# Down products of expert units 1 to 14, group 0: from four block products of 512 columns to seven products of sums of 256

## The chip, the cores and the metric

The kernel runs on one core of one Trainium2 chip. The metric is device microseconds (us) of one execution. TensorE (PE; PEld is its weight load) does the matrix products, VectorE (DVE), ScalarE (ACT) and GpSimd (POOL) work on rows of 128 partitions, and SyncE (SP) issues the transfers. PSUM is the memory that TensorE writes, in banks of 512 float32 columns.

## The reference, cut to what matters

A retention layer comes first, then a gated layer with 1536 hidden columns, then four experts with 1024 hidden columns each, all of whose outputs are summed with the weights `p`. The change is in the second product of the experts.

```python
def _moe2_ref(x, domain_probs, w1, w2):          # x: 1536 x 512, from the gated layer
    p = domain_probs / (domain_probs.sum(-1, keepdims=True) + 1e-09)
    out = np.zeros((N, D), dtype=np.float32)
    for e in range(E):                           # E = 4, F = 1024 hidden columns
        h = np.maximum(x @ w1[e], 0.0)
        out += p[:, e:e + 1] * (h @ w2[e])
    return out.astype(np.float32)
```

## The kernel before

The 1536 tokens are two groups `g` of 768, and a group is two blocks of 384 (three tiles of 128 tokens each). The 4 x 1024 hidden columns are 16 units `u` of 256, two parts `f` of 128. Every float32 operand is split into a high part `hi` (fp32r, rounded by a copy on ScalarE) and a low part `lo` (the rest, a subtraction on VectorE or GpSimd), and a product is three matmuls: hi x hi, hi x lo, lo x hi.

The expert stage walks through the steps (u, g). A step has two halves:

- `hidden_products` runs `winograd`: the hidden block of 256 columns x 768 tokens comes from seven products of sums in place of eight block products. Each is six matmuls of 384 columns (L463). They come in the order 1, 2, 5, 6, 3, 7, 4, and here they are p1, p2, p5, p6, p3, p7, p4. Products 1, 5 and 6 are copied out of PSUM (`kept`, L472, ScalarE), and the others are added to such a copy (L1036, VectorE). `expert_use` then makes the four operands `hs` by relu (L1039, L1027) with their low parts (L1043, L1029).
- `expert_out` makes the down product: six outputs of 128 tokens x 512 columns, each from two parts f by three matmuls of 512 columns (L1071 to L1073): 36 matmuls. VectorE adds each, times `p`, onto `oacc` (L1079).

A generator for the down product of a step (`before` in the last loop) is run between the products of the next step: p1, p2, three outputs, p5, p6, p3, p7, three outputs, p4. Thus TensorE's order is written out by hand. What the other engines do, and in which order, is set while the program is written by `Pace`: it holds assumed costs of each engine, and `fill` hands waiting tasks (level 0 first) to the engine that would be free; a task for `"PV"` may go to GpSimd or VectorE, and GpSimd is asked first. Each engine then executes its list strictly in order.

Weights: `piece_tasks` loads a piece into one of `STAGED` = 2 staging buffers, casts the high part (L380), and subtracts the low part (L385); for the up weights ("1", u) it also makes four sums (L352). Up weights take turns in three big places (`BIG`), the down weights ("2", u) have two small ones.

Of the kernel before, what the change touches and what calls it, by code (L numbers as in the profile page):

```python
# [15 lines left out]
P = 128  # L16
# [146 lines left out]
def tile_retention_gated_experts(  # L163
# [46 lines left out]
    N1 = DFF // FU  # L210
    UPE = F // FU
    N2 = E * UPE
    STAGED = 2
    BIG = 3
    SMALL = 2
    BANKS = 6
    WARM = 8

# [26 lines left out]


    pieces = []
    n_big = n_small = 0

    def wide(key, w, c0):  # L250
        nonlocal n_big
        rows = w.rearrange("(h j p) f -> j p h f", p=P, j=KH)
        for j in range(KH):
            pieces.append((key, j, rows[j, :, :, c0:c0 + FU], n_big))
        n_big += 1

    def plain(key, w, r0):
        nonlocal n_small
        for j in range(NF):
            pieces.append((key, j, w[r0 + j * P:r0 + (j + 1) * P, :].rearrange("p (h f) -> p h f", h=2), n_small))  # L260
            n_small += 1
# [14 lines left out]
    used = {"big": set(), "small": set()}  # L276
    pools = {}

    def is_wide(key):
        return key[0] in "gv1"  # L280

    def has_slot(n):
        key, j, _, slot = pieces[n]
        kind, size = ("big", BIG) if is_wide(key) else ("small", SMALL)
        pool = ("big", slot % BIG) if is_wide(key) else "small"
        return pool in pools and (slot < size or slot - size in used[kind])

    def w_used(key):
        kind = "big" if is_wide(key) else "small"
        used[kind].update(x[3] for x in pieces if x[0] == key)  # L290

    ready = {}
    open_weights = [False]
    stage_free, ones, tops, sums_done, highs = [], [[], []], [], [], []
    bits_pools = {0: psum_bits}

    def piece_tasks(n):

        key, j, src, slot = pieces[n]
        double = src.dtype == I64  # L300

        second = n % 2 if n >= 4 else 0
# [59 lines left out]

        def high_part(eng, half):
            if is_wide(key) and j == half == 0:
                assert has_slot(n)
                i = slot % BIG
                wt[key] = [
                    pools["big", i].tile([P, 7, KH, P], F32R, tag=f"big{part}{i}", name=f"wide{part}{i}", bufs=1)
                    for part in ("hi", "lo")
                ]  # L370
            elif not is_wide(key):
                assert has_slot(n)
                i = slot % SMALL
# [29 lines left out]
        for half in range(2 if is_wide(key) else 1):  # L403
            size = 384 if is_wide(key) and half == 0 else NC
            last = source
            if half == 1:
                for i in range(4):
                    before = sums_done[-1:] if i == 0 else []
                    last = then("PV", P, lambda eng, i=i: sums(eng, i), last, *before)
            hi = then(  # L410
                "A", size, lambda eng, half=half: high_part(eng, half), last, *highs[-1:], gate=lambda: has_slot(n)
            )
            highs.append(hi)
            lows.append(then("PV", size, lambda eng, half=half: low_part(eng, half), hi))
        if is_wide(key):
            sums_done.append(lows[-1])
        if double:
            tops[-1][0].extend(lows)
        stage_free.append(taken if double else lows)
        ready.setdefault(key, []).extend(lows)  # L420

    for n in range(len(pieces)):
        piece_tasks(n)

    def weights(key):
        pace.matmuls(0, pace.need(*ready[key]))
        return wt[key] if is_wide(key) else [wt[key + (f,)] for f in range(NF)]

    pools["big", 0] = pools["big", 1] = wring

# [493 lines left out]
    accp = ctx.enter_context(tc.tile_pool(name="accp", bufs=1))  # L924
    pools["big", 2] = inner

    turn = [0]

    def any_tile():

        n = turn[0] % 14
        turn[0] += 1
        if n < 4:
            silu_places.next()
            return tp.tile([P, TB], F32R, tag="s", name="hs", bufs=4)
        return pools["hp"].tile([P, TB], F32R, tag=("hhi", "hlo")[n % 2], name="hs")

    x2 = [None] * G
    x2_tasks = [{"X": [], "T": []} for _ in range(G)]
# [82 lines left out]

    def expert_use(hs):
        def use(f, blk, a, b):
            hi, lo = any_tile(), any_tile()
            if b is None:
                nc.scalar.activation(out=hi, in_=a, func=AF.Relu)  # L1027
                end = pace.did("A", TB)
                nc.vector.scalar_tensor_tensor(  # L1029
                    out=lo, in0=a, scalar=0.0, in1=hi.bitcast(F32), op0=ALU.max, op1=ALU.subtract  # L1030
                )
                end = pace.did("V", TB, end)
                hs[f, blk] = hi, lo, pace.done(end)
# [13 lines left out]
            readers += [high, low]  # L1047
            hs[f, blk] = hi, lo, low
            return end
        return use  # L1050

    def expert_out(u, g, hs):
        e = u // UPE
        w = weights(("2", u))
        if u == 0:
            oacc.append(accp.tile([P, 2 * CPB, DM], F32, tag=f"acc{g}", name=f"oacc{g}"))
        for n in range(2 * CPB):
# [8 lines left out]
            for half in range(halves):  # L1066
                cols = slice(half * DM // halves, (half + 1) * DM // halves)
                ps = bank()[:, cols]
                for f in range(NF):
                    (whi, wlo), (hi, lo, _) = w[f], hs[f, blk]  # L1070
# [12 lines left out]
                if u == N2 - 1:  # L1083
                    nc.sync.dma_start(out=out[tt * P:(tt + 1) * P, cols], in_=acc)
            if g == G - 1 and n == 2 * CPB - 1:
                w_used(("2", u))
            pace.fill(3 * NF * 0.216)
            yield

    first = {}  # L1090

    def hidden_products(u, g, hs):
        if u == 0:
            pace.matmuls(0, pace.need(*x2_tasks[g]["X"]))
        return winograd(weights(("1", u)), x2[g], expert_use(hs))

# [3 lines left out]
    for i, (u, g) in enumerate(steps):  # L1100
# [26 lines left out]
        if i == 5:  # L1127
            nc.vector.tensor_reduce(out=p_sum, in_=p_raw, axis=mybir.AxisListType.X, op=ALU.add)
            nc.vector.tensor_scalar(out=p_sum, in0=p_sum, scalar1=PEPS, scalar2=None, op0=ALU.add)
            nc.vector.reciprocal(out=p_sum, in_=p_sum)  # L1130
            nc.vector.tensor_tensor(out=p_sb, in0=p_raw, in1=p_sum.to_broadcast([P, NTT, E]), op=ALU.mult)
            pace.did("V", 300)
    for u in range(N2):
# [79 lines left out]
```

## Time and profile before

| | |
|---|---|
| time, median of 3 runs | 863.73 us (862.88 to 865.69) |
| profiled execution: its own time | 866.24 us |
| span of the profiled execution | 864.4 us, mean granted TensorE clock 1.000 |
| PE busy | 851.0 us (98%), 4731 matmul records |
| PEld busy | 792.9 us (92%) |
| DVE busy | 576.3 us (67%) |
| ACT busy | 379.7 us (44%) |
| POOL busy | 280.7 us (32%) |
| chain that ended last | 88% of the span on PE |

The span is first to last instruction on the core; the execution's own time is 1.8 us longer. Busy time of PE is modelled, so 98% does not say that it streams at its peak; the start times of its matmuls do say how fast they follow one another.

### The profile page before, as it was taken

The numbers are of one execution on the slowest core, as the hardware profiler recorded it, in microseconds if no ns is written. First come the engines' busy times: TensorE is split into PE (matmuls) and PEld (weight loads), VectorE is DVE, ScalarE is ACT, GpSimd is POOL, SyncE is SP. The second block draws the span as 40 slices with busy tenths as digits, with TensorE's granted clock in tenths as the row PEclk, the third lists the DMA queues.
The fourth block names the chain that finished last, engine by engine and source line by source line (L and its number), as shares of the span: only waits on it lengthen the run. The fifth ranks groups of instructions, "written<-read, shape, count | busy, mean of one in ns | idle before, by whom it ended". The sixth has DMA issues, their size and how long they took to land.

```text
span 864.4 us, 12619 instructions
## 1 busy us (share of the span) xinstructions
PE 851.0 (98%) x4731; PEld 792.9 (92%) x4731; DVE 576.3 (67%) x1054; ACT 379.7 (44%) x845; POOL 280.7 (32%) x354
## 2 busy tenths in 40 slices
PE   9989999999999999999999999999999999999998
PEld 8889999999999999889889998999899988999897
DVE  3987878979977876943665656556656556555554
ACT  3877765544344456655233233333233333333221
POOL 1366666525244458651122112012012112201000
PEclk9999999999999999999999999999999999999999
DMA  7762133221212111101011011001001101101003
GB/s 233 255 201 95 50 98 89 69 64 49 74 50 84 63 50 36 37 25 37 13 49 37 13 50 43 31 25 50 25 25 49 36 13 49 37 16 47 25 8 139
DMA packets 32749, 52.74 MB, mean 61 GB/s; under 512 B 4358, under 2 KB 13446, under 8 KB 32688
## 3 DMA queue, kind: packets, MB, share of 16 engines
q1 hardware_dynamic: 32480, 51.70, 19.1%
q8 instruction: 37, 0.61, 0.3%
q10 hardware_dynamic: 208, 0.23, 0.1%
q14 instruction: 24, 0.20, 0.1%
HBM read 48.78 MB, written 3.15 MB: 60 GB/s over the span
## 4 chain that ended last, share of the span: by engine, by line
PE 88%; DVE 5%; ACT 3%; POOL 2%; issue 2%; DVEq 0%; ACTq 0%; POOLq 0%
PE bank L463 41%; PE bank L1072 10%; PE bank L1073 10%; PE bank L1071 10%; PE bank L1004 3%; PE bank L1005 3%; PE bank L1003 3%; PE bank L676 2%; PE bank L668 1%; DVE s L556 1%; PE bank L648 1%; POOL x2Tlo L956 1%; DVE kept L553 1%; PE state L704 1%; PE bank L829 0%
## 5 line engine op out<-in xcount | busy, mean ns | idle before, releaser
L1079 DVE SCALAR_TENSOR_TENSOR oacc<-bank,p_sb,oacc 128x512 f32<-128x512 f32 (+1 forms) x181 | 135.0, 746 | 66.5 <-PE bank L1073 66.5
L1073 PE MATMUL bank<-plainhi,hs 128*128 128x512 f32 (+1 forms) x386 | 151.0, 391 | 0.0
L1072 PE MATMUL bank<-plainlo,hs 128*128 128x512 f32 (+1 forms) x386 | 151.0, 391 | 0.0
L1071 PE MATMUL bank<-plainhi,hs 128*128 128x512 f32 (+1 forms) x386 | 149.7, 388 | 0.0
L472 ACT COPY kept<-bank 128x384 f32<-128x384 f32 x168 | 80.8, 481 | 152.3 <-PE bank L463 150.4
L1036 DVE TENSOR_TENSOR kept<-bank,kept 128x384 f32<-128x384 f32 x96 | 53.5, 558 | 119.1 <-PE bank L463 94.9
L385 POOL TENSOR_TENSOR plainlo<-wst,plainhi 128x512 fp32r<-128x512 f32 x16 | 27.8, 1739 | 283.3 <-ACT plainhi L380 283.3
L463 PE MATMUL bank<-x2Thi,widehi 128*128 128x384 f32 x256 | 86.4, 338 | 0.7 <-DVE kept L1036 0.7
L463 PE MATMUL bank<-x2Thi,widelo 128*128 128x384 f32 x256 | 86.3, 337 | 0.0
L1073 PEld LDWEIGHTS bank<-plainhi,hs 128*128 128x128 f32 x386 | 72.5, 188 | 15.1
L463 PE MATMUL bank<-x2Tlo,widehi 128*128 128x384 f32 x256 | 86.0, 336 | 0.0
L1072 PEld LDWEIGHTS bank<-plainlo,hs 128*128 128x128 f32 x386 | 72.4, 187 | 14.1 <-POOL plainlo L385 0.3
L385 POOL TENSOR_TENSOR widelo<-sums,widehi 128x512 fp32r<-128x512 f32 x37 | 48.4, 1309 | 112.7 <-ACT widehi L380 112.3
L1071 PEld LDWEIGHTS bank<-plainhi,hs 128*128 128x128 f32 x386 | 72.5, 188 | 13.5
L1039 ACT ACTIVATE hs<-kept 128x384 fp32r<-128x384 f32 x96 | 50.6, 527 | 76.4 <-DVE kept L1036 76.4
L1004 PE MATMUL bank<-hlo,plainhi 128*128 128x384 f32 x192 | 64.4, 335 | 1.1 <-POOL hlo L561 1.0
L463 PE MATMUL bank<-xThi,widehi 128*128 128x384 f32 x192 | 64.6, 336 | 0.0
L463 PE MATMUL bank<-xThi,widelo 128*128 128x384 f32 x192 | 64.2, 334 | 0.0
L463 PE MATMUL bank<-xTlo,widehi 128*128 128x384 f32 x192 | 64.2, 334 | 0.0
L1005 PE MATMUL bank<-hhi,plainlo 128*128 128x384 f32 x192 | 64.2, 334 | 0.0
L1003 PE MATMUL bank<-hhi,plainhi 128*128 128x384 f32 x192 | 64.1, 334 | 0.0
L561 POOL TENSOR_TENSOR hlo<-s,hhi 128x384 fp32r<-128x384 f32 x44 | 47.0, 1071 | 33.4 <-ACT hhi L558 26.7
(155 smaller groups left out, 1925.9 us busy)
## 6 DMA issues: line engine op xcount, KB each, us to landing
wst<-in_moe_w_dram SPq DMA_DIRECT2D x64, 256.0 KB, 2.8
wst<-in_moe_w_gate_dram SPq DMA_DIRECT2D x12, 512.0 KB, 3.8
wst<-in_moe_w_val_dram SPq DMA_DIRECT2D x12, 512.0 KB, 3.7
wst<-in_moe_w_out_dram SPq DMA_DIRECT2D x12, 512.0 KB, 3.3
v<-in_vn_dram SPq DMA_DIRECT2D x12, 256.0 KB, 3.5
kn<-in_kn_dram SPq DMA_DIRECT2D x12, 256.0 KB, 3.9
q<-in_qt_dram SPq DMA_DIRECT2D x11, 256.0 KB, 4.4
k<-in_kt_dram SPq DMA_DIRECT2D x11, 256.0 KB, 3.1
```

Of the source, the lines that this page charges most:

```text
L385: eng.tensor_tensor(out=at(lo), in0=t, in1=at(hi).bitcast(F32), op=ALU.subtract)
L463: nc.tensor.matmul(out=ps, lhsT=lhs, rhs=rhs, start=(first and j == i == 0), stop=(j == KH - 1 and i == 2), skip_group_check=not first,)
L472: nc.scalar.copy(out=t, in_=ps)
L1003: nc.tensor.matmul(out=ps, lhsT=whi[:, c], rhs=hi, start=(f == 0), stop=False)
L1004: nc.tensor.matmul(out=ps, lhsT=whi[:, c], rhs=lo, start=False, stop=False)
L1005: nc.tensor.matmul(out=ps, lhsT=wlo[:, c], rhs=hi, start=False, stop=(f == NF - 1))
L1036: nc.vector.tensor_tensor(out=t, in0=a, in1=t, op=ALU.add)
L1039: 0, "A", TB, lambda eng: eng.activation(out=hi, in_=t, func=AF.Relu), [pace.done(end)]
L1071: nc.tensor.matmul(out=ps, lhsT=hi[:, c], rhs=whi[:, cols], start=(f == 0), stop=False)
L1072: nc.tensor.matmul(out=ps, lhsT=hi[:, c], rhs=wlo[:, cols], start=False, stop=False)
L1073: nc.tensor.matmul(out=ps, lhsT=lo[:, c], rhs=whi[:, cols], start=False, stop=(f == NF - 1))
L1079: nc.vector.scalar_tensor_tensor(out=acc, in0=ps, scalar=pe, in1=acc, op0=ALU.mult, op1=ALU.add)
```

## The change

The down product of group 0 is made by seven products of sums in units 1 to 14 (`MIXED`). The 256 x 512 down weights of a unit are four blocks of 128 x 256, the hidden block of 256 columns x 768 tokens four blocks of 128 x 384. Seven operands of hidden sums and seven of weights (four of them sums, `T`) are multiplied: for each product three tiles of 128 tokens, three matmuls each, of 256 columns. That is 63 matmuls of 256 columns in place of 36 of 512. The products are in the order 1, 4, 6, 5, 7, 3, 2; here they are m1, m4, m6, m5, m7, m3, m2. Group 1 and units 0 and 15 stay as they were.

Around it: `mixed_use` keeps the relu as float32 (`h`), makes four differences of such tiles, and splits seven operands in place of four. `down_sums` makes the four sums of down weights and splits them. `mixed_out` accumulates products in three banks and in two `cross` banks, which were used only for the weights' bits earlier, and adds each of the five partial results onto `oacc`, two of them in halves of 256 columns. After such a unit, TensorE takes the products of group 1's hidden block and the sums' products in turn, one of each (p1', m1, p2', m4, p5', m6, p6', m5, p3', m7, p7', m3, p4', m2; a dash marks group 1). There are three staging buffers, the third big place holds the down weights of odd units, up weights have two places, and down weights are loaded right behind the up weights of their own unit.

```diff
@@ constants and order of the loads
-    STAGED = 2
+    HD = DM // 2
+    MORE_HS = 2
+    MIXED = set(range(1, N2 - 1))
+    STAGED = 3
...
-    for u in range(N2):
-        turns += wides[2 * N1 + u + 1:2 * N1 + u + 2] + [plains[N1 + u]]
+    turns += [wides[2 * N1 + 1], plains[N1], plains[N1 + 1]]
+    for u in range(2, N2):
+        turns += [wides[2 * N1 + u], plains[N1 + u]]
...
@@ new: sums of the down weights
+        def sums(eng, i):
+            t1, t2, t3, t4 = tiles()
+            (b11, b12), (b21, b22) = of(upper), of(lower)
+            o, x, y = ((t1, b12, b11), (t2, b22, t1), (t3, b22, b12), (t4, b21, t2))[i]
+            eng.tensor_tensor(out=o, in0=x, in1=y, op=ALU.subtract)
...
@@ new: mixed_use, on group 0's hidden block
+        def operand(n, t, dep):
+            hi, lo, tags = pair()
+            high = pace.add(0, "A", TB, lambda eng: eng.copy(out=hi, in_=t), [dep])
+            low = pace.add(
+                0, "PV", TB, lambda eng: eng.tensor_tensor(out=lo, in0=t, in1=hi.bitcast(F32), op=ALU.subtract), [high]
+            )
...
+            elif at == (1, 1):
+                operand(4, t, done[at])
+                done[5] = sub(h[0, 1], h[0, 1], t, ALU.add, done[7], done[at])
+                done[6] = sub(h[0, 0], h[0, 1], h[0, 0], ALU.subtract, done[5], *read[1])
+                operand(5, h[0, 1], done[5])
+                operand(6, h[0, 0], done[6])
...
@@ new: mixed_out
+        plan = (
+            (1, plain_part(0, low_half), cross, lambda c: c != 1, (0, low_half, cross)),
+            (4, sum_part(3), left, lambda c: True, None),
+            (6, sum_part(1), cross, None, (0, high_half, cross)),
+            (5, sum_part(0), right, lambda c: False, (1, every, both)),
+            (7, sum_part(2), cross, None, (1, every, cross)),
+            (3, plain_part(1, high_half), right, None, None),
+            (2, plain_part(1, low_half), left, lambda c: True, (0, every, both)),
+        )
...
@@ the last loop
-            if not start:
+            if mixed:
+                hidden = hidden_products(u, g, hs, True)
+                for _ in range(7):
+                    next(hidden)
+                    next(before)
+            elif not start:
...
-            before = expert_out(u, g, hs)
+            mixed = is_mixed(u, g)
+            before = (mixed_out if mixed else expert_out)(u, g, hs)
```

What this does to the engines' lists is shown at three places of the steady stretch. First TensorE, between the last output of a down product and p4 of the next hidden block, before (L1071 to L1073 are an output's matmuls, L463 those of p4):

```order
L1071 MATMUL bank<-plainhi_7046,hs 128x512
L1072 MATMUL bank<-plainlo_7047,hs 128x512
L1073 MATMUL bank<-plainhi_7046,hs 128x512
L463 MATMUL bank<-x2Thi_4138,widehi_6553 128x384 [waits DVE_49]
L463 MATMUL bank<-x2Tlo_4139,widehi_6553 128x384
L463 MATMUL bank<-x2Thi_4138,widelo_6554 128x384
```

and now, from the end of p7' over m3 to the first matmul of p4' (L529 is the hidden products' line, L1231 that of the sums' products):

```order
L529 MATMUL bank<-x2Tlo_4144,widehi_7930 128x384
L529 MATMUL bank<-x2Thi_4143,widelo_7931 128x384
L1231 MATMUL bank<-plainhi_8074,hs 128x256 [waits DVE_49]
L1231 MATMUL bank<-plainlo_8075,hs 128x256
...
L1231 MATMUL bank<-plainhi_8074,hs 128x256 [waits DVE_49]
L1231 MATMUL bank<-plainlo_8075,hs 128x256
L1231 MATMUL bank<-plainhi_8074,hs 128x256
L529 MATMUL bank<-x2Thi_4143,widehi_7930 128x384 [waits DVE_49]
```

p4' writes the bank that p7' wrote, so it waits for VectorE's addition that reads it. Between p7 and p4 stood three outputs, 18 matmuls of 512 columns; between p7' and p4' stands m3, nine of 256.

Second, VectorE's list in the same stretch, now (the rows run from the additions of m5 to those of m2; L1208 is `mixed_out`'s addition, L1114 the addition onto `kept`, of p3' and then of p7', L1121 and L1107 low parts of group 1's operands):

```order
L1208 SCALAR_TENSOR_TENSOR oacc_4334<-bank,p_sb,oacc_4334 128x512 [waits PE_49] x2
L1114 TENSOR_TENSOR kept<-bank,kept 128x384 [waits DVE_49,PE_49,Activation_49]
L1208 SCALAR_TENSOR_TENSOR oacc_4334<-bank,p_sb,oacc_4334 128x512
L1208 SCALAR_TENSOR_TENSOR oacc_4334<-cross,p_sb,oacc_4334 128x512 [waits DVE_49,PE_49]
L1208 SCALAR_TENSOR_TENSOR oacc_4334<-cross,p_sb,oacc_4334 128x512 [waits DVE_49]
L1114 TENSOR_TENSOR kept<-bank,kept 128x384 [waits PE_49]
L1121 SCALAR_TENSOR_TENSOR hs<-kept,hs 128x384 [waits Pool_49]
L1121 SCALAR_TENSOR_TENSOR hs<-kept,hs 128x384 [waits Activation_49]
L1121 SCALAR_TENSOR_TENSOR hs<-kept,hs 128x384 [waits Activation_49,Pool_49]
L1107 SCALAR_TENSOR_TENSOR hs<-bank,hs 128x384 [waits Activation_49,Pool_49]
L1208 SCALAR_TENSOR_TENSOR oacc_4334<-cross,p_sb,oacc_4334 128x512
```

Three additions of 512 columns now stand between the addition for p3' and the one for p7'. Before, the two followed each other directly:

```order
L1079 SCALAR_TENSOR_TENSOR oacc_4468<-bank,p_sb,oacc_4468 128x512 [waits PE_49] x2
L1036 TENSOR_TENSOR kept<-bank,kept 128x384 [waits PE_49,Activation_49]
L1036 TENSOR_TENSOR kept<-bank,kept 128x384 [waits PE_49]
L1043 SCALAR_TENSOR_TENSOR hs<-kept,hs 128x384 [waits Activation_49]
L1079 SCALAR_TENSOR_TENSOR oacc_4468<-bank,p_sb,oacc_4468 128x512 [waits PE_49]
```

Third, GpSimd. Its whole list of a unit before is eight rows (`sums` and `widelo` belong to the up weights, `plainlo` to the down weights):

```order
L385 TENSOR_TENSOR widelo_6554<-sums,widehi_6553 128x4x128 [waits Activation_49]
L352 TENSOR_TENSOR sums<-wst 128x128 [waits DMAHW5_49,Pool_49]
L385 TENSOR_TENSOR widelo_6554<-wst,widehi_6553 128x2x128 [waits Activation_49]
L385 TENSOR_TENSOR widelo_6554<-wst,widehi_6553 128x128 [waits Activation_49]
L352 TENSOR_TENSOR sums<-sums,wst 128x128 [waits Pool_49]
L352 TENSOR_TENSOR sums<-wst 128x128
L352 TENSOR_TENSOR sums<-wst,sums 128x128 [waits Pool_49]
L385 TENSOR_TENSOR plainlo_6771<-wst,plainhi_6770 128x512 [waits DMAHW7_49,Activation_49]
```

Now it is 33 instructions, of which these rows are the part that ends before TensorE's m3 (L1143 differences of hidden tiles, L1137 low parts of the sums' operands):

```order
L1143 TENSOR_TENSOR h<-h 128x384 [waits Activation_49]
L1137 TENSOR_TENSOR hs<-h,hs 128x384 [waits Activation_49]
L1143 TENSOR_TENSOR h<-h 128x384 [waits Pool_49] x2
L1137 TENSOR_TENSOR hs<-h,hs 128x384 [waits Activation_49]
L1137 TENSOR_TENSOR hs<-h,hs 128x384 [waits PE_49,Activation_49]
L1137 TENSOR_TENSOR hs<-h,hs 128x384 [waits Activation_49]
L1137 TENSOR_TENSOR hs<-h,hs 128x384 [waits DVE_49,PE_49,Activation_49]
L1143 TENSOR_TENSOR h<-h 128x384 [waits Pool_49]
L400 TENSOR_TENSOR widelo_6197<-sums,widehi_6196 128x4x128
L1137 TENSOR_TENSOR hs<-h,hs 128x384 [waits DVE_49,PE_49,Activation_49]
L400 TENSOR_TENSOR plainlo_6338<-wst,plainhi_6337 128x512 x2
```

The other half of the weights' subtractions, which VectorE had before, is on GpSimd too; over all units GpSimd has 97 of the 98 low parts and 55 of the 56 differences. TensorE's list is the same as before up to the first of the sums' products; the lists of VectorE, ScalarE and GpSimd differ from the gated layer's products on, where the third staging buffer lets loads run ahead.

## Rows read from the trace of the kernel before

**Rows 1.** Busy time by stretch (PE, PEld, DVE, ACT, POOL; then clock, DMA share, GB/s).

```profile
200.00:300.00 100.00, 99.15 (x570) 98.22 (x569) 84.31 (x164) 45.42 (x100) 41.68 (x52) 1.00 0.22 69
300.00:395.00 95.00, 92.02 (x506) 88.18 (x505) 62.21 (x117) 55.34 (x120) 56.32 (x70) 1.00 0.11 34
...
405.00:835.00 430.00, 430.00 (x2155) 388.89 (x2154) 255.17 (x465) 142.65 (x297) 77.15 (x104) 1.00 0.11 33
```

**Rows 2.** Waits of TensorE's weight loads from 400 us on.

```profile
PEld bank L1072 <- POOL plainlo L385: 0.3, 1, 0.3
```

**Rows 3.** The chain that ended last, 578 to 612 us: start, duration, what.

```profile
578.68 4.18 PE bank L463 x24
582.87 0.23 PE bank L1071
...
586.99 3.14 PE bank L463 x18
...
609.83 2.28 PE bank L463 x13
```

**Rows 4.** TensorE's timeline at the end, matmuls of 256 columns (twelve in all).

```profile
859.48 0.28 PE L1071 MATMUL bank<-plainhi,hs 128*128 128x256 f32 x1
...
860.79 0.28 PE L1073 MATMUL bank<-plainhi,hs 128*128 128x256 f32 x1
```

**Rows 5.** Groups of VectorE by shape, 405 to 835 us (busy, mean ns, idle before).

```profile
L1079 DVE SCALAR_TENSOR_TENSOR oacc<-bank,p_sb,oacc 128x512 f32<-128x512 f32 x167 | 125.0, 749 | 60.2 <-PE bank L1073 60.2
L1036 DVE TENSOR_TENSOR kept<-bank,kept 128x384 f32<-128x384 f32 x83 | 46.3, 558 | 101.5 <-PE bank L463 77.3 <-ACT widehi L380 24.2
```

**Rows 6.** The same for VectorE, 850 us to the end.

```profile
L1079 DVE SCALAR_TENSOR_TENSOR oacc<-bank,p_sb,oacc 128x256 f32<-128x256 f32 x2 | 1.0, 484 | 0.2 <-PE bank L1073 0.2
```

**Rows 7.** VectorE's timeline near 701 us, two instructions back to back.

```profile
700.58 0.75 DVE L1079 SCALAR_TENSOR_TENSOR oacc<-bank,p_sb,oacc 128x512 f32<-128x512 f32 x1 [0.76 <-PE bank L1073]
...
701.25 0.55 DVE L1043 SCALAR_TENSOR_TENSOR hs<-kept,hs 128x384 fp32r<-128x384 f32 x1
```

**Rows 8.** Timelines near 707 us: a product's last matmul, the addition that reads it.

```profile
707.12 0.33 PE L463 MATMUL bank<-x2Thi,widelo 128*128 128x384 f32 x1
...
707.49 0.56 DVE L1036 TENSOR_TENSOR kept<-bank,kept 128x384 f32<-128x384 f32 x1 [0.41 <-PE bank L463]
707.97 0.55 DVE L1043 SCALAR_TENSOR_TENSOR hs<-kept,hs 128x384 fp32r<-128x384 f32 x1
```

**Rows 9.** Timelines near 367 us: p4 waits for the addition of p7.

```profile
366.58 0.56 DVE L1036 TENSOR_TENSOR kept<-bank,kept 128x384 f32<-128x384 f32 x1
...
367.19 0.44 PE L463 MATMUL bank<-x2Thi,widehi 128*128 128x384 f32 x1 [0.65 <-DVE kept L1036]
367.47 0.34 PE L463 MATMUL bank<-x2Tlo,widehi 128*128 128x384 f32 x1
367.65 0.34 PE L463 MATMUL bank<-x2Thi,widelo 128*128 128x384 f32 x1
```

**Rows 10.** Groups of GpSimd by shape, 405 to 835 us.

```profile
L385 POOL TENSOR_TENSOR plainlo<-wst,plainhi 128x512 fp32r<-128x512 f32 x13 | 23.5, 1804 | 236.1 <-ACT plainhi L380 236.1
L385 POOL TENSOR_TENSOR widelo<-sums,widehi 128x512 fp32r<-128x512 f32 x13 | 16.7, 1286 | 89.5 <-ACT widehi L380 89.5
L352 POOL TENSOR_TENSOR sums<-wst 128x128 f32<-128x128 f32 x26 | 12.0, 460 | 1.0
L385 POOL TENSOR_TENSOR widelo<-wst,widehi 128x256 fp32r<-128x256 f32 x13 | 9.7, 743 | 0.0
L385 POOL TENSOR_TENSOR widelo<-wst,widehi 128x128 fp32r<-128x128 f32 x13 | 6.0, 465 | 0.0
```

**Rows 11.** Groups of GpSimd by shape, 100 to 350 us.

```profile
L561 POOL TENSOR_TENSOR hlo<-s,hhi 128x384 fp32r<-128x384 f32 x39 | 41.4, 1063 | 32.4 <-ACT hhi L558 25.7 <-PE bank L463 4.5 <-issue 2.2
...
L956 POOL TENSOR_TENSOR x2Tlo<-x2acc,x2Thi 128x384 fp32r<-128x384 f32 x5 | 5.7, 1140 | 0.0
```

**Rows 12.** Groups of VectorE by shape, 100 to 350 us.

```profile
L556 DVE TENSOR_TENSOR s<-kept,s 128x384 f32<-128x384 f32 x32 | 24.3, 760 | 1.1
...
L556 DVE TENSOR_TENSOR s<-bank,s 128x384 f32<-128x384 f32 x10 | 5.5, 547 | 0.2 <-PE bank L463 0.2
```

More of the change, by code (lines that the diff above doesn't have):

```diff
@@ L280, in is_wide, with has_slot @@
         return key[0] in "gv1"
[L282 to L290, printed above, removed]
+    def has_slot(key):
+        return place_of[key] in pools and (former[key] is None or former[key] in used)
+    w_used = used.add
     ready = {}
     open_weights = [False]
+    sums_used, halves = set(), {}
     stage_free, ones, tops, sums_done, highs = [], [[], []], [], [], []
@@ L297, in piece_tasks @@
     def piece_tasks(n):
-        key, j, src, slot = pieces[n]
+        key, j, src = pieces[n]
+        place = place_of[key]
         double = src.dtype == I64
@@ L364, in high_part @@
             if is_wide(key) and j == half == 0:
-                assert has_slot(n)
-                i = slot % BIG
+                assert has_slot(key)
+                i = place[1]
                 wt[key] = [
-                    pools["big", i].tile([P, 7, KH, P], F32R, tag=f"big{part}{i}", name=f"wide{part}{i}", bufs=1)
+                    pools[place].tile([P, 7, KH, P], F32R, tag=f"big{part}{i}", name=f"wide{part}{i}", bufs=1)
                     for part in ("hi", "lo")
                 ]
+            elif not is_wide(key) and place != "small":
+                assert has_slot(key)
+                if j == 0:
+                    i = place[1]
+                    wt[key] = [
+                        pools[place].tile([P, 7, KH, P], F32R, tag=f"big{part}{i}", name=f"plain{part}{i}", bufs=1)
+                        .rearrange("p a k f -> p (a k f)") for part in ("hi", "lo")
+                    ]
+                wt[key + (j,)] = [t[:, j * DM:(j + 1) * DM] for t in wt[key]]
             elif not is_wide(key):
-                assert has_slot(n)
-                i = slot % SMALL
+                assert has_slot(key)
+                i = j
                 wt[key + (j,)] = [
@@ L418, in piece_tasks, with down_sums, of, tiles @@
             tops[-1][0].extend(lows)
+        if key[0] == "2" and key[1] in MIXED:
+            halves[j] = got, source, lows
+            if j == NF - 1:
+                down_sums(key[1], then)
         stage_free.append(taken if double else lows)
         ready.setdefault(key, []).extend(lows)
+    def down_sums(u, then):
+        (upper, dep0, free0), (lower, dep1, free1) = halves[0], halves[1]
+        key, got, lows = ("T", u), {}, []
+        def of(which):
+            t = which["t"].rearrange("p h f -> p (h f)")
+            return t[:, 0:HD], t[:, HD:DM]
+        def tiles():
+            if "t" not in got:
+                got["t"] = [wconv.tile([P, 512], F32, tag="top", name="down") for _ in range(2)]
+            return [t[:, x * HD:(x + 1) * HD] for t in got["t"] for x in range(2)]
+        def sums(eng, i):
[3 more added lines that the diff above has]
+            eng.tensor_tensor(out=o, in0=x, in1=y, op=ALU.subtract)
+        def high(eng, half):
+            if half == 0:
+                wt[key] = [
+                    pools["T"].tile([P, 4, HD], F32R, tag=f"T{part}", name=f"down{part}", bufs=1) for part in ("hi", "lo")
+                ]
+            eng.copy(out=wt[key][0][:, 2 * half:2 * half + 2].rearrange("p n d -> p (n d)"), in_=got["t"][half])
+        def low(eng, half):
+            hi, lo = (w[:, 2 * half:2 * half + 2].rearrange("p n d -> p (n d)") for w in wt[key])
+            eng.tensor_tensor(out=lo, in0=got["t"][half], in1=hi.bitcast(F32), op=ALU.subtract)
+        gate = lambda: "T" in pools and (u == min(MIXED) or u - 1 in sums_used)
+        last = dep1
+        steps = []
+        for i in range(4):
+            before = tops_free[-1:] if i == 0 else []
+            last = then("PV", HD, lambda eng, i=i: sums(eng, i), last, dep0, *[x for b in before for x in b])
+            steps.append(last)
+        free0 += [steps[0], steps[2]]
+        free1 += steps[1:]
+        for half in range(2):
+            hi = then("A", 512, lambda eng, half=half: high(eng, half), steps[2 * half + 1], gate=gate)
+            lows.append(then("PV", 512, lambda eng, half=half: low(eng, half), hi))
+        tops_free.append(lows)
+        ready[key] = lows
@@ L1086, in expert_out @@
                 w_used(("2", u))
+            if n in (CPB - 1, 2 * CPB - 1):
+                for f in range(NF):
+                    leave(hs[f, blk][3])
             pace.fill(3 * NF * 0.216)
@@ L1090, in tile_retention_gated_experts, with is_mixed, hidden_products @@
     first = {}
-    def hidden_products(u, g, hs):
+    def is_mixed(u, g):
+        return g == 0 and u in MIXED
+    def hidden_products(u, g, hs, fine=False):
         if u == 0:
             pace.matmuls(0, pace.need(*x2_tasks[g]["X"]))
-        return winograd(weights(("1", u)), x2[g], expert_use(hs))
+        use = mixed_use(hs) if is_mixed(u, g) else expert_use(hs)
+        return winograd(weights(("1", u)), x2[g], use, fine)
     before = iter(())
```

142 lines of the change are left out of this document (123 added, 19 removed).

## The prediction

> **What bounds the kernel now.** I read the busy times by stretch first. From 405 to 835 us, the expert stage, PE is busy all of 430.00 us, and VectorE 255.17, ScalarE 142.65 and GpSimd 77.15 [rows 1]. Busy time alone would not show that TensorE never waits, so the list of its waits comes next: from 400 us to the end one wait of 0.3 us [rows 2]. Here the length of TensorE's own stream is the time, and whatever shortens it shortens the kernel, if nothing new makes it wait. The chain then gives the stream's parts. Two steps, that is one unit, take 609.83 - 578.68 = 31.15 us; 24 matmuls of 384 columns take 4.18 us, 0.174 each; three outputs (18 matmuls of 512 columns) take 586.99 - 582.87 = 4.12 us, 0.229 each [rows 3]. A step's hidden block is 42 x 0.174 = 7.32 us, its down product 36 x 0.229 = 8.24 us.
>
> **The change part by part.** *TensorE.* In each of 14 units 36 matmuls of 512 columns go and 63 of 256 come. The trace has twelve of that shape, in the last output: from the first to the last, eleven steps, 860.79 - 859.48 = 1.31 us, 0.119 us each [rows 4]. The columns fall from 18,432 to 16,128, an eighth, but the time falls less: at a granted clock of 1.00 [rows 1], the level of 2.4 GHz, 256, 384 and 512 columns stream in 0.107, 0.160 and 0.213 us, so each matmul carries 0.012 to 0.016 us more, and there are now more matmuls. So 63 x 0.119 = 7.50 us replace 8.24: 0.74 us a unit. I use 0.1195 for the pitch, since those twelve ran beside idle engines, hence 7.53, a gain of 0.71 us a unit and 9.9 us in all. The row bounds the pitch from below; from above I take the spread of the 512-column pitch in the same chain (0.23 to 0.24), 3%: 0.123 us, which leaves 0.49 us a unit, 6.9 us in all.
>
> The Trainium skill, "TensorE: Matmul & The Clock Gate", section on the back-to-back issue gap, puts 256 columns at 262 cycles of 2.4 GHz, 109 ns, and by that the gain would be 14 x (8.24 - 6.87) = 19 us, an estimate. Its section on LDWEIGHTS puts a load of 128 columns at 107 ns, as long as the 256 columns stream. The trace has 119 ns with loads included, and the sum goes by that.
>
> *New waits on TensorE.* Count time from the start of p1'. A hidden product is 6 x 0.174 = 1.05 us, a product of sums 9 x 0.1195 = 1.08. In turn: m4 starts at 3.17, m6 at 5.29, m5 at 7.41, p3' ends at 9.54, m7 at 10.61, p7' at 11.66, m3 at 12.73. p4' writes p7's bank, so it waits for VectorE's addition of p7'. An addition starts 0.37 us after the start of the last matmul that it reads and the next instruction can start 0.48 after it [rows 8]; for 512 columns the next starts after 0.67 [rows 7]. The addition for p3' starts at 9.74; then the list has one addition of m5 and two of m7, to 10.22 + 3 x 0.67 = 12.23; the addition for p7' starts there, and not at 11.86, and ends at 12.79 with 0.56 [rows 5]. Where p4 waited for such an addition before, it started 0.05 after that ended, and its first matmul took 0.28 where others take 0.17 [rows 9]. So p4' starts at 12.84, 0.11 late, and loses 0.11 more: 0.22 us a unit, 3.1 us in all. Below, it is nothing, if additions from `cross` are a little shorter; above, 0.75 in place of 0.67 for three additions gives 0.46 us a unit, 6.4 us. Behind the p7' addition stand group 1's low parts, the last addition of m7 and those of m2; they are wanted by the first output at 17 us, over 3 us later.
>
> *VectorE in all.* A unit had 255.17 / 430 x 31.15 = 18.5 us of it. Now: 6 additions of 256 at 0.48 [rows 6], 15 of 512 at 0.75, ten of 384 at 0.56 [rows 5], 19.7 us of 30.4. The weights' subtractions that it loses pay for the additions that it gains.
>
> *ScalarE in all.* 10.3 us of a unit before [rows 1]; seven more copies of 384 and two of 512, at no more than VectorE's 0.56 and 0.75, make that under 16 of 30.4. It stays half idle, so I cost it at nothing.
>
> *GpSimd* gets the work. A unit had 5.6 us; now it has 11 tiles of 384, 4 sums of 256, 8 of 128, and the low parts of all weights. At the durations of the stage, 0.74 for 256, 0.46 for 128, 1.29 for 512 [rows 10] and 1.06 for 384 [rows 11]: 11.7 + 3.0 + 3.7 + 2.4 (up weights, parts of 256 and 128) + 6 x 1.29 = 28.5 us of the new 30.4. It is nearly full, but in order it has room: sub and low parts for m4 and m6 can start after p7 of group 0, some 5 us before p1'; counted down its list, the one for m4 ends about 2.5 us after p1' starts (wanted at 3.17), m6's at 4.5 (wanted at 5.29), m3's at 8.8 (wanted at 11.66). So I cost it at nothing. If that cover of 0.7 us goes, all that is later goes onto TensorE, once a unit.
>
> *Weights, buffers.* Transfers fill an 11% share of the DMA in this stage [rows 1], and the same pieces are loaded. Up weights have two places; a place is free at the end of the unit that read it, a whole unit of 30 us before its next use, against some 4 us of casts and subtractions. Nothing. In the gated layer TensorE's list is the same, but the order on the others shifts with the third buffer. There it stands idle for 0.85 us in 200 to 300 and 2.98 in 300 to 395 [rows 1]; a new order can win or lose some of that, which I take as 0, from -2 to +2.
>
> *Sum.* -9.9 + 3.1 = -6.8 us. The profiled execution took 866.24 us, 2.5 over the median of the runs; against its own time that is 859.4, against the median 863.73 - 6.8 = 856.9. I say 857.0.
>
> **Rivals.** *A. VectorE's and GpSimd's latencies eat the gain.* p4' loses 0.46 instead of 0.22, and m4 or m6 waits some 0.2 to 0.3 us for a low part: 14 x 0.7 = 9.9 us, 863.7, no change. For it: the two margins above are 0.7 us at best, in lists with over 30 instructions. Against: most waits of the lists have more than 2 us.
>
> *B. GpSimd becomes the bound, and the kernel is slower.* From 31.15 us of GpSimd a unit (work and its own waits) the old period is passed, and every further 0.1 us is 1.4 us. Place: the operands' low parts, for which m4 and m6 wait. The rows have an upper price: 1.14 for 384 [rows 11] and 1.80 for the 512 of staged weights [rows 10] make 12.5 + 3.0 + 3.7 + 2.4 + 2 x 1.29 + 4 x 1.80 = 31.4, and with 1 us of waits in its list 32.4: 14 x 1.25 = 17.5 us slower, 881. For it: VectorE's additions with two tiles from SBUF took 0.76 where those with one from PSUM took 0.55, while GpSimd was 42% busy [rows 1, 12], and the 1.80 stood beside VectorE's own half of the same weights. The Trainium skill, "SBUF — State Buffer", section on who interferes with whom, says why: a VectorE instruction with two SBUF inputs and a GpSimd instruction that reads SBUF lock one port in turn, each for the whole instruction. By that rule a fuller GpSimd delays and is delayed; the rows agree in sign. Against: that half of the weights has left VectorE, so the 1.80 should fall to 1.29, and only three or four of VectorE's instructions a unit still have two SBUF inputs. Also, sums of GpSimd's durations overstate it a little.
>
> *C. The sums' matmuls follow more slowly than 0.119,* for example since two products' banks are read while their neighbours are written: 0.123 takes 3 us, and the forecast becomes 860. It stays on the faster side.
>
> **Numbers.** Forecast with C, from 851.9 (no p4' wait, and 2 us won earlier) to 861.1: 0.63. A, from 861.1 to 866.3: 0.20. B, slower than that: 0.17. 0.3%, 2.6 us, is about what a measurement of this kernel can tell from no change. Faster 0.64, within it 0.19, slower 0.17. The range for 8 in 10 runs from 852.5 to 866.5: under 0.05 lies below, and of B some 0.15 above. The likeliest case's own range is 853 to 861.
>
> **What the next profile would show.** Right: steps of 256 columns 0.119 to 0.123 apart; one unit 30.4 to 30.8 us; one short wait of p4' for VectorE's addition a unit, about 0.1 us; no wait of the sums' products for GpSimd; GpSimd over 85% busy in the stage and VectorE at about 65%. Wrong: waits of PEld on L1137 (GpSimd) or L1135 (ScalarE) at m4, m6 or m5 in each unit (A or B), plain weights' low parts still at 1.8 us (B), a pitch above 0.125 (C further than I allow), or over 2 us of new idle time of TensorE before 395 us.

## The result, and the profile after

The changed kernel takes 856.1 us (median, 854.15 to 856.44), the kernel before 863.69 beside it: a ratio of 0.9904, 95% interval 0.9881 to 0.9927. The forecast was 857.0, and faster.

Busy time by stretch, after (columns as in [rows 1]; the expert stage is shorter now, so the window ends earlier):

```profile
200.00:300.00 100.00, 99.92 (x575) 99.28 (x574) 84.55 (x162) 47.05 (x104) 46.47 (x59) 1.00 0.22 68
300.00:395.00 95.00, 90.89 (x499) 86.88 (x498) 54.81 (x101) 54.90 (x119) 65.35 (x80) 1.00 0.11 33
405.00:826.00 421.00, 421.00 (x2517) 398.18 (x2516) 254.40 (x434) 193.37 (x415) 349.62 (x427) 1.00 0.11 33
```

PE is still busy throughout the expert stage. GpSimd has gone from 18% (77.15 of 430, [rows 1]) to 83%, ScalarE from 33% to 46%, VectorE stays at 60%. The end of this window, behind GpSimd's last work for the sums, lowers its share; in one whole unit GpSimd is busy for 26.87 of 30.59 us, 88%:

```profile
583.00:613.59 30.59, 30.59 (x185) 28.93 (x184) 18.18 (x31) 14.35 (x32) 26.87 (x34) 1.00 0.12 35
```

The waits of the weight loads from 400 us on hold one line, where [rows 2] had another:

```profile
PEld bank L529 <- DVE kept L1114: 2.0, 12, 0.2
```

This is p4' waiting for the addition of p7', in 12 of 14 units, and no line names GpSimd. The chain of one unit (start, duration, what), against [rows 3]:

```profile
581.64 2.10 PE bank L529 x12
583.75 1.07 PE cross L1231 x9
584.82 1.04 PE bank L529 x6
585.86 1.07 PE bank L1231 x9
...
594.31 1.06 PE bank L1231 x9
595.38 1.29 PE bank L529 x6
596.67 1.07 PE bank L1231 x9
597.74 2.08 PE bank L529 x12
...
603.95 4.18 PE bank L529 x24
```

Nine matmuls of 256 columns take 1.07 us. Between neighbours of this line, all over the stage, the mean step is 0.1183 us (784 pairs). A hidden product takes 1.04, but p4' (from 595.38) 1.29. VectorE's timeline there shows why:

```profile
592.29 0.56 DVE L1114 TENSOR_TENSOR kept<-bank,kept 128x384 f32<-128x384 f32 x1 [0.40 <-issue]
592.77 0.74 DVE L1208 SCALAR_TENSOR_TENSOR oacc<-bank,p_sb,oacc 128x512 f32<-128x512 f32 x1
593.42 1.40 DVE L1208 SCALAR_TENSOR_TENSOR oacc<-cross,p_sb,oacc 128x512 f32<-128x512 f32 x2
594.74 0.55 DVE L1114 TENSOR_TENSOR kept<-bank,kept 128x384 f32<-128x384 f32 x1
```

Between the additions of p3' and p7' stand the three of 512 columns, back to back; the addition for p7' ends at 594.74 + 0.55 = 595.29. TensorE's timeline at the same place, from the last matmul of m3 to the second of p4':

```profile
595.10 0.28 PE L1231 MATMUL bank<-plainhi,hs 128*128 128x256 f32 x1
595.35 0.44 PE L529 MATMUL bank<-x2Thi,widehi 128*128 128x384 f32 x1
595.62 0.33 PE L529 MATMUL bank<-x2Tlo,widehi 128*128 128x384 f32 x1
```

p4' starts 0.25 behind the start of the last matmul of m3 where 0.12 is usual, and its first step is 0.27 where 0.17 is: 0.13 late, 0.10 lost behind it.

To see where time went, I cut each profiled execution at the start of three matmuls: the first of the gated layer's down product, the first of the experts' first down output, and the last of all. Stretches in us, worked out from the timelines, good to about 0.2 (the kernels of the experiments stand here too):

| | up to the gated down product | to the first expert output | to the last matmul |
|---|---|---|---|
| before | 102.7 | 269.1 | 489.0 |
| after | 102.0 | 268.1 | 480.9 |
| after, run again | 102.1 | 268.1 | 481.0 |
| m2 ahead of p4' | 101.9 | 268.1 | 478.0 |
| no sums | 102.3 | 268.0 | 489.0 |
| order of loads of before | 101.8 | 267.3 | 580.0 |
| the same, no sums | 102.3 | 267.3 | 489.1 |
| two staging buffers | 98.8 | 270.0 | 481.5 |
| GpSimd + 2 / + 4 | 99.7 / 102.1 | 268.1 / 268.1 | 481.8 / 500.1 |
| m2 ahead of p4', unit 15 too | 101.7 | 268.1 | 478.1 |
| VectorE first, experts | 99.7 | 270.4 | 525.0 |
| VectorE first, gated | 100.1 | 267.4 | 478.0 |

Of the 9.9 us between the two profiled executions (before's 866.24, after's 856.38) 8.1 lie in the expert stage, 1.0 in the gated layer, and 0.7 at the start, a stretch that spreads by 4 us over the kernels of the table. So stages are compared by the last two columns. The executions of both kernels lie at two levels (beside the changed kernel run again: before 863.5 and 866.0 us, changed 854.0 and 856.6, all means), so that the gain is 9.4 us from level to level, and only 7.6 between the two medians above, the one of the lower and the other of the upper level.

### The profile page after: what moved, and what is told of

Its sections match the earlier page's. It is cut to its first block, busy times and chain, and to the rows that moved or that the text cites. A ratio compares the mean times of both kernels' runs of the same rounds, so it can differ in the third digit from the quotient of the medians.

```text
span 854.6 us, 13897 instructions
## 1 busy us (share of the span) xinstructions
PE 842.6 (99%) x5109; PEld 804.2 (94%) x5109; DVE 567.2 (66%) x1010; ACT 433.2 (51%) x971; POOL 576.2 (67%) x706
## 4 chain that ended last, share of the span: by engine, by line
PE 90%; DVE 4%; ACT 3%; POOL 2%; issue 1%; DVEq 0%; ACTq 0%; POOLq 0%
PE bank L529 44%; PE bank L1231 7%; PE bank L1269 6%; PE bank L1270 6%; PE bank L1268 6%; PE cross L1231 5%; PE bank L1082 3%; PE bank L1083 3%; PE bank L1081 3%; PE bank L742 2%; PE bank L734 1%; PE bank L714 1%; POOL x2Tlo L1034 1%; PE state L770 1%; DVE s L622 1%
## 5 line engine op out<-in xcount | busy, mean ns | idle before, releaser
L1208 DVE SCALAR_TENSOR_TENSOR oacc<-cross,p_sb,oacc 128x256 f32<-128x256 f32 (+1 forms) x126 | 65.6, 565 | 64.2 <-PE cross L1231 64.2
L1276 DVE SCALAR_TENSOR_TENSOR oacc<-bank,p_sb,oacc 128x512 f32<-128x512 f32 (+1 forms) x97 | 72.3, 745 | 51.9 <-PE bank L1270 51.8
L1137 POOL TENSOR_TENSOR hs<-h,hs 128x384 fp32r<-128x384 f32 x97 | 97.7, 1026 | 0.7 <-ACT hs L1135 0.6
L529 PE MATMUL bank<-x2Thi,widehi 128*128 128x384 f32 x256 | 87.8, 343 | 0.7 <-DVE kept L1114 0.7
L529 PE MATMUL bank<-x2Thi,widelo 128*128 128x384 f32 x256 | 86.1, 336 | 0.0
L529 PE MATMUL bank<-x2Tlo,widehi 128*128 128x384 f32 x256 | 85.9, 336 | 0.0
L1270 PE MATMUL bank<-plainhi,hs 128*128 128x512 f32 (+1 forms) x218 | 85.1, 390 | 0.0
L1269 PE MATMUL bank<-plainlo,hs 128*128 128x512 f32 (+1 forms) x218 | 85.0, 390 | 0.0
L1268 PE MATMUL bank<-plainhi,hs 128*128 128x512 f32 (+1 forms) x218 | 84.3, 387 | 0.0
L1117 ACT ACTIVATE hs<-kept 128x384 fp32r<-128x384 f32 x54 | 28.4, 525 | 86.9 <-DVE kept L1114 86.9
L529 PE MATMUL bank<-xThi,widehi 128*128 128x384 f32 x192 | 64.5, 336 | 0.0
L529 PE MATMUL bank<-xThi,widelo 128*128 128x384 f32 x192 | 64.2, 334 | 0.0
L529 PE MATMUL bank<-xTlo,widehi 128*128 128x384 f32 x192 | 64.2, 334 | 0.0
L400 POOL TENSOR_TENSOR widelo<-sums,widehi 128x512 fp32r<-128x512 f32 x45 | 58.6, 1303 | 7.8 <-ACT widehi L395 6.1
L1208 DVE SCALAR_TENSOR_TENSOR oacc<-bank,p_sb,oacc 128x512 f32<-128x512 f32 x84 | 59.1, 744 | 6.4 <-PE bank L1231 6.4
L470 POOL TENSOR_TENSOR downlo<-down,downhi 128x512 fp32r<-128x512 f32 x28 | 36.3, 1299 | 37.4 <-ACT downhi L466 37.4
L1143 POOL TENSOR_TENSOR h<-h 128x384 f32<-128x384 f32 x55 | 56.1, 1019 | 4.2 <-ACT h L1156 2.2
```

The costliest lines, as they stand in the source:

```text
L529: nc.tensor.matmul(out=ps, lhsT=lhs, rhs=rhs, start=(first and j == i == 0), stop=(j == KH - 1 and i == 2), skip_group_check=not first,)
L1137: 0, "PV", TB, lambda eng: eng.tensor_tensor(out=lo, in0=t, in1=hi.bitcast(F32), op=ALU.subtract), [high]
L1208: run = lambda eng: eng.scalar_tensor_tensor(out=acc, in0=ps, scalar=pe, in1=acc, op0=ALU.mult, op1=ALU.add)
L1276: nc.vector.scalar_tensor_tensor(out=acc, in0=ps, scalar=pe, in1=acc, op0=ALU.mult, op1=ALU.add)
```

## The experiments

Ratios are to the kernel before, run beside each kernel.

**The changed kernel again.** 

> The changed kernel itself, as the measure for the kernels of this call. All theories: 0.988 to 0.993 of the kernel before, its unit 30.6 us.

Measured: 856.46 us (853.95 to 856.84), ratio 0.9894 (0.9877 to 0.9911). It is the measure for the next three.

**m2 ahead of p4'.**

```diff
-                for _ in range(7):
+                for _ in range(6):
                     next(hidden)
                     next(before)
+                next(before)
+                next(hidden)
```

> The last two products of the interleave change places: m2, then p4'. Theory: the only wait of the sums' stage is p4' for VectorE's addition of p7', 0.12 us late and about 0.10 lost behind it; with m2 between them the wait goes, a unit takes 30.4 us in place of 30.6, and the kernel is 2 to 3 us faster than the changed one (853 to 854.5 us). Rival: the chain of VectorE's additions is what limits, and the wait comes back at p1 or the first output of the next step: the same time as the changed kernel, 856.

Measured: 852.54 us (851.40 to 853.38), ratio 0.9856 (0.9838 to 0.9874). TensorE has no wait at all from 400 us on, and in the chain m3 and m2 stand together, with p4' at its full pace in the three hidden products behind them:

```profile
591.99 1.04 PE bank L529 x6
593.03 2.15 PE bank L1231 x18
595.18 3.12 PE bank L529 x18
```

The unit falls from 30.59 to 30.37 us (13 steps from one unit's first sums to the next), by the 0.22 of the forecast; the expert stage by 2.9 us. The wait comes back at no other place: the rival, that the chain of VectorE's additions limits, did not happen.

**No products of sums**, all the rest of the change kept.

```diff
-    MIXED = set(range(1, N2 - 1))
+    MIXED = set()
```

> No unit has products of sums; three staging buffers, the new order of the loads and the new places stay. Theory: the gain is TensorE's, 12 to 14 units of 0.55 us each, and at most 2 us come from the rest: 861.5 to 864 us, a unit of 31.1 us. Rival: a good part of the gain comes from the loads and the buffers (the first 395 us and a shorter stream behind them): below 860 us.

Measured: 863.76 us, ratio 0.9989 (0.9978 to 1.0001). The expert stage is that of before to 0.1 us; the gated layer keeps what the changed kernel wins there (1.1 us here, 1.0 in the changed kernel). So the products of sums are the gain of the expert stage, and the rest of the change is worth about 1 us by the stages; the ratio alone does not tell it from nothing.

**The order of the loads of before**, all the rest of the change kept.

```diff
-    turns += [wides[2 * N1 + 1], plains[N1], plains[N1 + 1]]
-    for u in range(2, N2):
-        turns += [wides[2 * N1 + u], plains[N1 + u]]
+    for u in range(N2):
+        turns += wides[2 * N1 + u + 1:2 * N1 + u + 2] + [plains[N1 + u]]
```

> The changed kernel with the loads in the order of before (a unit's down weights behind the up weights of the next unit). Theory: loads are far ahead of their use, no change against the changed kernel, within 1.5 us. Rival: the order of loads decides when GpSimd makes the sums of the down weights, and m4 to m7 wait for them or the low parts of the hidden sums come late: 3 us or more slower than the changed kernel, with waits of TensorE on GpSimd in the sums' stage.

Measured: 953.08 us, ratio 1.1022 (1.1000 to 1.1045). My theory was wrong by almost 100 us. The waits of TensorE's weight loads from 395 us on:

```profile
PEld bank L1230 <- DVE downlo L469: 62.9, 13, 5.0
PEld cross L1230 <- DVE plainlo L399: 2.7, 12, 0.2
PEld bank L1230 <- ACT downhi L465: 1.5, 1, 1.5
```

The low part of the sums of down weights comes 5 us late, once a unit. Busy time through one unit (columns as above; the last three are the granted clock, the DMA share and GB/s):

```profile
595.50:598.00 2.50, 2.17 (x9) 2.17 (x10) 1.40 (x3) 0.00 (x0) 1.32 (x2) 0.50 0.00 0
598.00:599.80 1.80, 1.80 (x7) 1.80 (x7) 0.00 (x0) 0.00 (x0) 0.00 (x0) 0.50 0.00 0
599.80:611.50 11.70, 11.70 (x82) 11.68 (x81) 9.07 (x16) 3.27 (x8) 0.00 (x0) 0.99 0.01 1
611.50:629.00 17.50, 17.18 (x90) 15.19 (x88) 10.12 (x14) 10.16 (x23) 17.25 (x22) 1.00 0.16 48
629.00:632.00 3.00, 0.00 (x0) 0.00 (x0) 3.00 (x6) 1.03 (x2) 2.87 (x3) 0.80 0.28 81
```

GpSimd does nothing from 599.8 to 611.5 and has no gap from there until TensorE stops. Over 450 to 826 us it is busy 60% of the time, less than in the changed kernel, and is still in the way. ScalarE's timeline has the start of it:

```profile
610.73 0.48 ACT L537 COPY kept<-bank 128x384 f32<-128x384 f32 x1 [1.62 <-PE bank L528]
611.11 0.61 ACT L394 CAST widehi<-wst 128x256 fp32r<-128x256 f32 x2
```

The next up weights are cast as soon as the unit before has left their place (there are two places now). The casts follow the order of the loads, so the down weights of the running unit come behind them: their four sums share GpSimd with the differences and low parts of the hidden sums, all in the 17.5 us between the cast and m4. The last step of the delay stands on VectorE's list: the low part `downlo`, whose input ScalarE cast at 623.2, is behind a difference that waits for GpSimd:

```profile
628.59 1.33 DVE L1142 TENSOR_TENSOR h<-h 128x384 f32<-128x384 f32 x1 [0.91 <-POOL hs L1136]
...
631.56 1.80 DVE L469 TENSOR_TENSOR downlo<-down,downhi 128x512 fp32r<-128x512 f32 x2
```

The unit takes 37.55 us in place of 30.59. Of the 6.96, 4.8 are the wait for `downlo` (62.9 / 13) and 0.2 that for `plainlo`; the rest, some 2 us, fits the clock, which stands at 0.50, the level of 1.2 GHz, for some 4 us behind the idle time. There 256 columns follow each other in 0.21 us and 384 in 0.32.

**The same, without the sums** (both diffs above).

> The order of the loads of before with the new places, as in the run that took 953 us, but no unit has products of sums. Theory (that loss came from GpSimd's work for the sums, squeezed behind the late up weights): with only the weights' own low parts left nothing is late, 862 to 866 us. Rival (two places for up weights and this order of loads are too slow by themselves): over 880 us, with waits of TensorE on the plain weights.

Measured: 863.97 us, ratio 0.9995 (0.9979 to 1.0011), and TensorE's weight loads have no wait at all from 400 us on. The theory holds: that order with two places is harmless alone, and costs 97 us with the sums. That GpSimd's part of the sums' work does it is read from the trace above. The converse, that order with the sums and three places for up weights, was not tried.

**More work on GpSimd.** The additions double a spare tile and give nothing to the result. There are two of them a unit in the first kernel (shown) and four in the second.

```diff
+    spare = extra.tile([P, 512], F32, name="spare")
+    nc.gpsimd.memset(spare, 0.0)
...
+            if n == 3:
+                for _ in range(2):
+                    nc.gpsimd.tensor_tensor(out=spare, in0=spare, in1=spare, op=ALU.add)
```

> The changed kernel with two additions of 512 columns more on GpSimd in each unit of sums, at m3 in its list; they add up a spare tile and give nothing to the result. At the 1.3 us of such an instruction in this stage they are 2.6 us a unit. Theory (GpSimd has room): it stands idle 2.9 us a unit behind the casts of the sums of the down weights, so the work fits and the time stays within 2 us of the changed kernel. Rival (GpSimd's list is already the length of a unit, TensorE is only ahead by what was prepared): 2 us or more a unit, 28 us or more in all.

> The same with four additions, 5.2 us a unit. Theory: GpSimd's 25.4 us of work a unit and these are 30.6, as long as the unit, and not all of its waits for ScalarE go: it becomes the bound, a unit of 31 to 33 us, 6 to 30 us slower than the changed kernel, with waits of TensorE for the low parts of the sums' operands. Rival (GpSimd's waits all give way): no more than 2 us slower.

Measured: two additions 857.12 us, ratio 0.9914 (0.9890 to 0.9938), not to be told from the changed kernel, with GpSimd busy for 380.56 of 421 us, 90%; four 875.68, ratio 1.0132 (1.0108 to 1.0157). In the changed kernel, GpSimd's waits in the stage are led by the first line below; with two additions it is the second. With four it is gone, and TensorE's waits (third line) and the busy time (fourth) show who is the bound:

```profile
POOL downlo L470 <- ACT downhi L466: 37.4, 13, 3.6
```

```profile
POOL downlo L470 <- ACT downhi L466: 8.5, 13, 2.1
```

```profile
PEld cross L1233 <- POOL hs L1139: 17.5, 10, 1.8
```

```profile
405.00:826.00 421.00, 404.98 (x2412) 381.32 (x2412) 250.44 (x411) 185.14 (x406) 412.83 (x479) 1.00 0.11 33
```

The place is m6, whose third matmul waits for its operand's low part, the third of four that GpSimd makes in a row. A unit with four additions takes 30.6 to 31.2 us at first and 32.43 later on. There GpSimd's list runs without a stop, so without the four additions (1.07 each) it is 28.2 us long: some 2.4 us under the changed kernel's unit of 30.59. That is the distance to rival B, measured.

**VectorE asked ahead of GpSimd** in the expert stage; the line stands ahead of the last loop, where the order was "DPAV".

```diff
+    pace.order = "DVPA"
```

> In the expert stage the planner asks VectorE ahead of GpSimd, so that VectorE has nearly all low parts and differences and GpSimd little but weights. Theory (VectorE's list, with the additions that free the banks, is the one that must not grow): VectorE goes from 60% to over 85% busy, its additions come late, TensorE waits at p4' and at the sums' products, and the kernel is 5 us or more slower than the changed one. Rival (GpSimd at 1.03 us for a low part is the engine that holds things up, VectorE does it in 0.55): the same time or faster.

Measured: 901.27 us, ratio 1.0432 (1.0408 to 1.0456). In the stage VectorE is busy 363.17 of 421 us (86%), and TensorE waits 33.7 us, 12 times, ahead of the sums' products in `cross`. The list of waits names nothing that ends them, but the chain runs through VectorE's `h` and `hs` (L1143, L1137) there and ends with an addition from `cross` (L1208). VectorE is the engine that must keep room. Its longer list and rows of it that take longer beside GpSimd's are not separated: shortly before one such wait ends, this difference takes 1.19 us where others take 0.56.

```profile
605.07 1.19 DVE L1143 TENSOR_TENSOR h<-h 128x384 f32<-128x384 f32 x1
```

GpSimd's groups of this kernel (first two) and of the changed one (last two):

```profile
L400 POOL TENSOR_TENSOR plainlo<-wst,plainhi 128x512 fp32r<-128x512 f32 x12 | 48.6, 4052 | 155.8 <-ACT plainhi L395 155.8
L459 POOL TENSOR_TENSOR down<-wst 128x256 f32<-128x256 f32 x12 | 12.5, 1043 | 0.0
```

```profile
L400 POOL TENSOR_TENSOR plainlo<-wst,plainhi 128x512 fp32r<-128x512 f32 x28 | 36.2, 1313 | 0.0
L459 POOL TENSOR_TENSOR down<-wst 128x256 f32<-128x256 f32 x24 | 17.8, 742 | 0.0
```

**m2 ahead of p4' (the edit shown above), and unit 15 with sums too** (its group 0 output isn't stored in this kernel, so its time lacks those transfers).

```diff
-    MIXED = set(range(1, N2 - 1))
+    MIXED = set(range(1, N2))
```

> m2 ahead of p4' as before, and the last unit (15) has products of sums in group 0 too. Theory: one more unit at the gain of the others without a wait, 8.24 us less 63 matmuls of 0.1183, 0.79 us: 851.7 us. Rival: the last unit has no next unit behind which its additions can lie, and gives nothing: 852.5.

Measured: 853.07 us, ratio 0.9869 (0.9847 to 0.9890): no gain. The profile has one new wait, 0.8 us of TensorE for VectorE's addition onto `oacc` (L1208), as long as the gain would be.

**Two staging buffers.**

```diff
-    STAGED = 3
+    STAGED = 2
```

> The changed kernel with two staging buffers in place of three. Theory (the third buffer keeps the loads going while a unit's two halves of down weights wait for their four sums): without it the up weights of the next unit start later, GpSimd's work bunches and TensorE waits in the sums' stage, 5 us or more slower than the changed kernel. Rival: transfers take some 3 us and the stage has 30 us a unit for six of them, so two buffers do: within 2 us of the changed kernel.

Measured: 859.19 us (855.60 to 860.82), ratio 0.9940 (0.9920 to 0.9960), slower than the changed kernel by some 3 us, between the theories. TensorE's waits from 400 us on come to 1.2 us, less than in the changed kernel, and the expert stage is 0.6 us longer; the gated layer is 1.8 us longer, from this stretch on:

```profile
200.00:300.00 100.00, 99.14 (x570) 98.22 (x568) 83.59 (x160) 47.43 (x103) 41.85 (x52) 1.00 0.21 64
```

PE and PEld read as in before [rows 1], where the changed kernel has 99.92 and 99.28. So without the third buffer the gain in the gated layer is gone. The two stages are 2.4 us longer together, most of the 3. The edit also moves work: VectorE is busy for 286.06 us from 405 to 826 us where it was 254.40, GpSimd for 294.96 where it was 349.62.

**VectorE first in the last unit of the gated layer**, with m2 ahead of p4' (shown above). The second line stands ahead of the last loop.

```diff
+        if u == N1 - 1:
+            pace.order = "DVPA"
...
+    pace.order = "DPAV"
```

> m2 ahead of p4', and in the last unit of the gated layer the planner asks VectorE ahead of GpSimd. TensorE still waits 2.4 us for low parts by GpSimd (hlo) and 1.9 us for x2Xlo by VectorE there. Theory: the first wait goes, the second stays, about 2 us faster than 852.5. Rival: VectorE is the busier engine in that stretch, the work on x2 comes later for it, and TensorE waits longer: 3 us or more slower than 852.5.

Measured: 851.24 us (850.55 to 852.49), ratio 0.9849 (0.9820 to 0.9877), the fastest, but by the ratios not to be told from m2 alone. The wait for hlo falls from 2.4 to 0.8 us, that for x2Xlo grows from 1.9 to 2.8; the gated stretch is 0.7 us shorter. The other 1.8 us by which this profile is ahead lie in the start, which the edit doesn't touch.

## Why the prediction was right

*The gain on TensorE* was forecast with a pitch of 0.1195 us as 0.71 us a unit; the pitch is 0.1183, so 8.24 - 63 x 0.1183 = 0.79 us, and the unit without the wait, 30.37, is 0.78 below before's 31.15. Rival C (0.123) did not happen. The 0.109 that the Trainium skill gives for the isolated gap, without the weight load ("TensorE: Matmul & The Clock Gate", back-to-back issue gap), is not reached: the trace has 0.118 with each matmul's own weights loaded.

*The wait of p4'* was forecast at 0.22 us a unit: 0.11 late, 0.11 behind. The trace has 0.13 and 0.10, and moving m2 gave back 0.22. VectorE's list has the three additions ahead of it, as the forecast had it.

*GpSimd at no cost.* The forecast had 28.5 us a unit, and over 85% busy; the run with four additions measures 28.2, and the whole unit above 26.87, 88%. The forecast rested on two low parts, for m4 and m6, ending 0.7 and 0.8 us before their use. GpSimd's timeline in the unit above has four low parts in one row, and TensorE's has m6:

```profile
583.43 3.95 POOL L1137 TENSOR_TENSOR hs<-h,hs 128x384 fp32r<-128x384 f32 x4
...
587.81 0.28 PE L1231 MATMUL cross<-downhi,hs 128*128 128x256 f32 x1
```

The third of them, m6's, ends by 583.43 + 3 x 0.99 = 586.4, and m6 starts at 587.81: 1.4 us, nearly twice the forecast's margin. The one for m4 stands ahead of this row (with four additions, m4's last matmul starts at 657.75 and the row only at 657.89). It ends here at 580.39 + 1.02 = 581.41, before p1' starts at 582.55 and not 2.5 us behind that, so the tighter of the two margins was 4.3 us. That the plain weights' 1.80 us [rows 10] would fall came true, 1.31. The reason given, that VectorE's half of them is gone, is not shown to be it: in the run without sums, where VectorE has its half again, GpSimd's takes 1.35 (the last section has the rows). VectorE took 18.2 us of the whole unit and not 19.7 (60% of the stage and not 65%), ScalarE 14.4, under the 16 of the forecast.

*The gated layer* was forecast at 0, from -2 to +2; it gave -1.0.

*The sum.* 14 x 0.79 less 14 x 0.22 is 8.0 us, and the expert stage is 8.1 shorter; the forecast had 6.8, short by the 1.1 us of the pitch. With the gated layer's 1.0 the two stages gave 9.1. That 857.0 is only 0.9 from the measured median is in part luck: against the 9.4 from level to level, the forecast's 6.8 is 2.6 short.

*What the forecast had not seen.* "Weights, buffers" was costed at nothing by comparing 30 us between uses with 4 us of work. The result agrees, but only for the new order of loads, of which the forecast said nothing: that this term came out right is luck. The order of before is 89 us slower than the kernel before, five times the price of rival B. What counts is not whether a place is free a unit ahead, but what stands behind its first user in GpSimd's list.

## What to carry to other kernels

When products are traded for sums, count the engine that makes the sums in the window between its last input and its first use, not over the period: GpSimd at 60% came too late in the old order of the loads, and at 90%, with two additions, was in time in the new one. Put a product that waits for a reader of its bank one place later: changing the order of independent products cost nothing here and gave 2.9 us. Compare stages between fixed points of the trace; here the first 100 us alone spread by 4 us.

## What the hardware showed that I had not expected

A subtraction of 512 columns on GpSimd takes 1.31 us in the changed kernel, and 4.05 us when VectorE, 86% busy, makes sums and low parts from two tiles in SBUF at the same time. VectorE's low parts of 384 columns (L1137) take 0.56 there, its differences (L1143) 0.71. The Trainium skill, "SBUF — State Buffer", section on who interferes with whom, says that a VectorE instruction with two SBUF inputs and a GpSimd instruction that reads SBUF contend for a shared port, which is an exclusive lock. The rows agree. In that run GpSimd has most of the delay, but not in all: here are the two halves of a unit's plain weights, first in the kernel before and then in the run without sums.

```profile
712.28 0.68 DVE L385 TENSOR_TENSOR plainlo<-wst,plainhi 128x512 fp32r<-128x512 f32 x1
712.32 1.80 POOL L385 TENSOR_TENSOR plainlo<-wst,plainhi 128x512 fp32r<-128x512 f32 x1 [18.17 <-ACT plainhi L380]
...
586.13 1.29 POOL L400 TENSOR_TENSOR plainlo<-wst,plainhi 128x512 fp32r<-128x512 f32 x1 [5.57 <-ACT plainhi L395]
586.29 1.68 DVE L400 TENSOR_TENSOR plainlo<-wst,plainhi 128x512 fp32r<-128x512 f32 x1
```

In both pairs the half that starts first keeps its time, and the other takes 0.5 or 1.0 us longer.

A wait of TensorE cost more than itself: behind 5 us of idle time the granted clock was 0.50 from 595.5 to 599.8 us, some 2 us more a unit. With VectorE first, behind a wait of 2.52 us, it was 0.50 from 541.5 to 544.0 us, and 0.97 over the stage. In the run with four additions, with waits of at most 1.8 us, it stayed at 1.00.
